# Plain v issued from ScalarE's DMA queue, with a newly searched fixed order, in a fused attention and gated-unit kernel

## The chip, the cores and the metric

The kernel runs on one core of a Trainium2 chip. The metric is the time of one execution on the device, in microseconds. Before the change it is 174.27 us, the median of 3 runs (173.8 to 174.28).

## The reference

Attention over 8 batches, 8 heads, 576 positions and a head width of 64, then a gated unit on its output. Heads 0 to 3 look at the 32 last positions ("plain"), heads 4 to 7 at every fourth of the last 128 ("dilated").

```python
scores = scale * np.matmul(q, k.transpose(0, 1, 3, 2))
mask_plain = (rel >= 0) & (rel < window)
mask_dil = (rel >= 0) & (rel < window * dilation) & (rel % dilation == 0)
...
attn = attn / (np.sum(attn, axis=-1, keepdims=True) + 1e-09)
return np.matmul(attn, v).astype(np.float32)
...
for k in range(K):
    gate_pre += conv_w[k][None, None, :] * xp[:, k:k + S, :]
gate = 1.0 / (1.0 + np.exp(-gate_pre))
val = x @ w_val
return (gate * val @ w_out).astype(np.float32)
```

x is the attention's output with its heads side by side (512 wide), xp the same with K - 1 = 4 rows of zeros ahead, so the gate is a causal convolution of 5 taps in each channel.

## The kernel before, in words

The kernel is a list of 733 tasks, each a handful of instructions of one engine. It is built by `dilated`, `plain`, `gated`, `outputs` and `weights`; no scheduler runs at build time. The string ORDER gives the order of all tasks: an entry such as 34A is task 34 on ScalarE; P is TensorE, V VectorE, G GpSimd, S SyncE. Every engine executes its own entries in that order and waits in order: an instruction that waits holds up all behind it. A number behind the P (33P6) is a count of warm-up matmuls of 512 columns (L659) that are issued ahead of the task. HOMES says which buffer of its class each tensor gets. Both strings were made offline by a planner with assumed costs for each task; the kernel only replays them.

The tasks of one batch b, for the dilated and the plain half:

| name | engine | what |
|---|---|---|
| Lqd, Lkd, Lvd, Lqp, Lkp | SyncE | loads of q, k, v, 576 to 768 KB each |
| Lvp (L302) | SyncE | load of plain v into a buffer vp (two of them), in rows of 64 floats, 256 bytes; 576 KB for batches 0 to 3, 768 KB for 4 to 7 |
| Tqd, Tkd, Tqp, Tkp | TensorE | transposes of q and k to PSUM (L464, L401) |
| Eqd, Ekd, Eqp, Ekp | ScalarE or VectorE | their copies to SBUF (L312, L314) |
| Sd, Sp; Ed, Ep; Md, Mp | TensorE; ScalarE; VectorE | scores (L333), exponential (L340), mask (L347) |
| U | GpSimd or ScalarE | cast of dilated v, vd to vn, 1536 elements a partition (L316) |
| HA, HB, HC, HD | GpSimd or ScalarE | casts of plain v, vp to vw, moved to other partitions: 2, 3, 3 and 2 instructions (batches 0 to 3 only; L316, L312) |
| Ad, Ap; Nd, Np | TensorE; VectorE | attention times v (L356), division by the sum (L365, L366) |
| Xd, Xp; Fd, Fp | TensorE; ScalarE or VectorE | transposes of the result, copies into xT |

For each pair of batches follow the gated unit in 3 or 4 blocks: C (the convolution as matmuls with diagonal matrices, L530), G (its tanh on ScalarE), V (times w_val, L548), Y (VectorE); then 36 output tiles O (times w_out, L577) with their eviction EO and store ST (SyncE). w_val and w_out are loaded as FP32 and cast on GpSimd by Wv and Wo (two tasks for w_out: Wo1, Wo0); O0 needs both. `weights` also makes conv_diag, the identity times conv_w (L616).

Loads on SyncE are kept short by DEPTH = 5: a big load waits until the big load five places earlier has landed.

```python
if t.load:
    t.after = big[-DEPTH] if len(big) >= DEPTH else None
    if t.big:
        big.append(t)
```

Task numbers used below: 49, 114, 203 are Lvp of batches 0, 1, 2; 17 is Lvd and 18 U of batch 0 (U0); 50 to 53 are HA to HD of batch 0, 204 to 207 those of batch 2 (HA2 to HD2); 66 and 76 are the two Ap of batch 0; 178, 181, 190 and 193 the four Ed of batch 2; 209 and 210 the two Eqp of batch 2; 12 and 10 are Wo1 and Wo0; 221 and 231 the two Np of batch 2; 625 is O0.

Of the kernel before, what the change touches and what calls it, by code (L numbers as in the profile page):

```python
# [31 lines left out]
388P 389A 358P 296V 360A 311P 312A 361P 363A 333V 359V 287P 362V 288V 297P 337P 298A 338V 385S 417S 374P 375A
319P 386S 320A 307P 308A 353P 351P 639S 377P 364P 354V 376V 313P 357S 469S 642S 416S 352A 378A 379V 365A 402P
321P 390P 314V 403V 407P 367P 322V 649P 366V 368A 391A 380P 309P 485P 408A 650A 381V 369V 310V 404P 392P 393A
405A 486V 646P 370P 647A 422P 419P 394V 371V 424V 423A 421A 645S 470S 651S 633S 502S 418S 655P 382P 438P 409V
395P 420A 439A 387G 396A 315P 316A 449P 656A 383V 406V 410P 652P 411V 450A 435P 531S 425P 372P 653A 436A 426A
# [672 lines left out]
```

## Time and profile before

| | us | share of the span |
|---|---|---|
| median of 3 runs | 174.27 | |
| the profiled execution | 173.37 | |
| its span, first to last instruction | 171.7 | |
| TensorE (PE) busy | 153.0 | 89% |
| VectorE (DVE) busy | 121.7 | 71% |
| ScalarE (ACT) busy | 108.4 | 63% |
| GpSimd (POOL) busy | 44.2 | 26% |
| DMA: packets' time of 16 engines | | 82.2% |
| granted TensorE clock | 0.998 | |

The profile is of one execution. Busy time leaves out the instructions that issue a DMA; a row "SPq ... DMA_DIRECT2D" tells when SyncE took up an issue and for how long. A share of the DMA engines above 1 means that packets overlap on an engine. In a group's row stand the line, engine, operation, what is written and read with shapes, the count, the busy time in us, the mean of one in ns, and the idle time of the engine ahead of it with what ended most of it.

### The profile page before, as it was taken

To read this page: it belongs to the slowest core of one execution; us is meant where nothing else is said; L and a number is where in the kernel's file an instruction comes from. 1 tells how busy PE (TensorE), PEld (TensorE's weight loads), DVE (VectorE), ACT (ScalarE), POOL (GpSimd) and SP (SyncE) were. 2 spreads that over 40 slices of the span, in tenths; PEclk is the share of its full clock that TensorE was granted. 3 is DMA by queue.
4 is the path that set the end of the run, shared out by engine and by line. 5 is a ranking of instruction groups with operands and counts; after the bars stand their busy time and mean duration, and the time that the engine had idled before them with its cause. 6 is when DMAs were issued, how large, how long until landed. Compare 5 with 4: busy or idle time off the path is not lost.

```text
span 171.7 us, 5752 instructions
## 1 busy us (share of the span) xinstructions
PE 153.0 (89%) x2441; PEld 102.2 (60%) x2460; DVE 121.7 (71%) x243; ACT 108.4 (63%) x182; POOL 44.2 (26%) x82
## 2 busy tenths in 40 slices
PE   6697967888989979899999799989999999999990
PEld 1355654677557546567766567576656577666640
DVE  6549778989899579779788658899368776664220
ACT  2147976198868744798847693888946675242542
POOL 7023998560659427403000000210110000000000
PEclk9999999999999999999999999999999999999999
DMA  4999999999799999999994948969979060333445
GB/s 137 325 355 290 375 370 210 311 374 319 200 383 364 362 269 281 373 353 222 282 328 139 267 115 286 373 165 390 270 202 303 2 244 4 116 119 138 186 165 199
DMA packets 49123, 43.63 MB, mean 254 GB/s; under 512 B 22981, under 2 KB 39365, under 8 KB 49098
## 3 DMA queue, kind: packets, MB, share of 16 engines
q1 hardware_dynamic: 49098, 43.27, 82.2%
q8 instruction: 19, 0.31, 0.7%
q14 instruction: 6, 0.05, 0.1%
HBM read 33.83 MB, written 9.44 MB: 252 GB/s over the span
## 4 chain that ended last, share of the span: by engine, by line
PE 58%; DMA 12%; DVE 11%; ACT 6%; SPq 5%; issue 3%; POOL 3%; ACTq 0%; DVEq 0%; POOLq 0%
PE pu L577 17%; PE pd L548 14%; PE pd L530 9%; DMA qk<-in_k_dram 5%; PE pd L356 5%; DVE et L347 4%; DMA wt<-in_moe_w_out_dram 4%; SPq L281 4%; PE pd L333 4%; DMA qk<-in_q_dram 3%; PE pu L464 3%; POOL w_out L316 3%; PE pd L401 2%; PE pu L488 2%; ACT et L340 2%
## 5 line engine op out<-in xcount | busy, mean ns | idle before, releaser
L340 ACT ACTIVATE et<-pd 128x576 bf16<-128x576 f32 x64 | 39.3, 657 | 10.4 <-PE pd L333 9.3
L347 DVE TENSOR_TENSOR et<-et,mask 128x576 bf16<-128x576 bf16 x64 | 33.9, 557 | 4.7 <-ACT et L340 4.5
L548 PE MATMUL pd<-xT,w_val 128*128 128x384 bf16 (+1 forms) x208 | 34.9, 313 | 0.7 <-DVE xn L366 0.4
L577 PE MATMUL pu<-w_out,yT 128*128 128x512 bf16 x127 | 33.4, 379 | 1.4 <-issue 0.6
L558 DVE SCALAR_TENSOR_TENSOR yT<-gate,pd 128x768 bf16<-128x768 bf16 (+1 forms) x26 | 23.0, 886 | 12.5 <-PE pd L548 8.5
L366 DVE TENSOR_TENSOR xn<-pd,rec 96x768 bf16<-96x768 f32 x32 | 30.5, 954 | 1.1
L316 POOL CAST vn<-vd 128x1536 bf16<-128x1536 f32 x8 | 12.3, 1540 | 70.3 <-DMA vd<-in_v_dram 70.3
L540 ACT ACTIVATE gate<-pd 128x768 bf16<-128x768 f32 (+1 forms) x26 | 19.9, 769 | 10.9 <-DVE yT L558 5.5
L548 PEld LDWEIGHTS <-w_val 128*128 128x128 bf16 x208 | 19.4, 97 | 11.6 <-issue 1.5
L530 PE MATMUL pd<-xT,conv_diag 64*64 64x384 bf16 (+1 forms) x520 | 23.1, 313 | 1.8 <-DVE xT L314 1.1
L584 ACT ACTIVATE osb<-pu 128x512 f32<-128x512 f32 x27 | 16.2, 601 | 11.0 <-PE pu L577 10.7
L577 PEld LDWEIGHTS <-yT 128*128 128x128 bf16 x144 | 12.6, 97 | 13.3 <-issue 1.1
L333 PE MATMUL pd<-qT,kT 64*128 64x96 bf16 x384 | 16.1, 209 | 3.1 <-ACT qT L312 0.9
L530 PEld LDWEIGHTS <-conv_diag 64*64 64x64 bf16 x520 | 15.1, 106 | 6.2 <-issue 2.5
L316 POOL CAST vw<-vp 32x384 bf16<-32x384 f32 (+2 forms) x31 | 16.8, 541 | 7.5 <-DMA vp<-in_v_dram 6.1
L356 PEld LDWEIGHTS <-et 128*128 128x128 bf16 x384 | 14.7, 97 | 6.5 <-DVE et L347 2.5
L464 PE MATMUL pu<-ident,qk 128*128 128x128 bf16 x160 | 14.8, 230 | 3.0 <-DMA qk<-in_k_dram 2.0
L333 PEld LDWEIGHTS <-kT 64*128 64x128 bf16 x384 | 10.1, 96 | 11.5 <-issue 6.3
L464 PEld LDWEIGHTS <-qk 128*128 128x128 bf16 x160 | 10.8, 102 | 7.3 <-DMA qk<-in_k_dram 3.0
L314 DVE COPY xT<-pu 128x576 bf16<-128x576 bf16 x18 | 10.1, 568 | 4.0 <-PE pu L488 3.1
L312 ACT COPY xT<-pu 128x576 bf16<-128x576 bf16 x14 | 8.9, 646 | 6.2 <-PE pu L428 3.6
L365 DVE RECIPROCAL rec<-pd 96x12 f32<-96x12 f32 x32 | 7.1, 223 | 7.6 <-PE pd L356 4.5
(52 smaller groups left out, 146.2 us busy)
## 6 DMA issues: line engine op xcount, KB each, us to landing
out_dram<-osb SPq DMA_DIRECT2D x36, 256.0 KB, 2.7
vd<-in_v_dram SPq DMA_DIRECT2D x8, 768.0 KB, 9.3
qk<-in_k_dram SPq DMA_DIRECT2D x8, 576.0 KB, 7.8
qk<-in_q_dram SPq DMA_DIRECT2D x8, 576.0 KB, 8.0
qk<-in_q_dram SPq DMA_DIRECT2D x6, 640.0 KB, 9.1
qk<-in_k_dram SPq DMA_DIRECT2D x6, 640.0 KB, 8.7
vp<-in_v_dram SPq DMA_DIRECT2D x4, 768.0 KB, 7.9
vp<-in_v_dram SPq DMA_DIRECT2D x4, 576.0 KB, 9.8
```

The costliest lines, as they stand in the source:

```text
L316: nc.gpsimd.tensor_copy(out_, in_)
L333: nc.tensor.matmul(out=ps2[ps.idx][:, l, QB * jj:QB * jj + QB], lhsT=kT[kt.idx][rb, c:c + 128], rhs=qT[qt.idx][rb, c:c + QB], start=True, ...
L340: nc.scalar.activation(out=et[e.idx][:, 0:2 * HW].rearrange("p (l n) -> p l n", l=2), in_=ps2[ps.idx][:, :, 0:HW], func=AF.Exp, scale=scale)
L347: (nc.vector if eng == DVE else nc.gpsimd).tensor_tensor(out=ev, in0=ev, in1=m, op=ALU.mult)
L356: nc.tensor.matmul(out=ps2[po.idx][:, hf, (2 * jj + l) * DA:(2 * jj + l + 1) * DA], lhsT=et[es[hf].idx][:, c:c + 128], rhs=val(j, l), star ...
L366: nc.vector.tensor_tensor(out=xn[xt.idx][0:QB].rearrange("p (h j) l d -> p h (j l) d", h=2), in0=a[:, :, :, 0:D], in1=rr[:, :, :, None].to ...
L464: nc.tensor.transpose(out=o[:, f:f + 128], in_=a[:, c * RD + 128 * cb:c * RD + 128 * cb + 128], identity=ident)
L530: nc.tensor.matmul(out=dst(ps2[pc.idx][64 * ob:64 * ob + 64, n, 0:wd]), lhsT=conv_diag[rb, 2 * cp + n, kk, :], rhs=mov(2 * cp + n, rb, c0 ...
L540: nc.scalar.activation(out=gate[gt.idx][:, :, 0:wd], in_=ps2[pc.idx][:, :, 0:wd], func=AF.Tanh, scale=0.5)
L548: nc.tensor.matmul(out=dst(ps2[pv.idx][:, n, 0:wd]), lhsT=w_val[:, mc, c * 128:(c + 1) * 128], rhs=mov(mc, slice(0, 128), c0), start=(mc = ...
L558: nc.vector.scalar_tensor_tensor(out=yT[yb.idx][:, 2 * cp:2 * cp + 2, t0:t0 + wd], in0=gate[gt.idx][:, :, 0:wd], scalar=1.0, in1=ps2[pv.id ...
L577: nc.tensor.matmul(out=ps1[po.idx], lhsT=yT[yb.idx][:, c, c0:c0 + 128], rhs=w_out[:, c, :], start=(c == 0), stop=(c == NCH - 1))
```

## The change

Plain v is issued by `nc.scalar.dma_start` on ScalarE instead of SyncE, so an Lvp is an entry of ScalarE (49A, 114A, 203A) and stands in ScalarE's order. It no longer counts in the list behind DEPTH, and has no DEPTH wait of its own. ORDER and HOMES are new. The last numbers in SHIFTS, planned costs of the casts HA to HD, go from 1.0 and 1.45 to 1.1 and 1.65; they act through ORDER only. conv_w becomes FP32. New tasks K (the convolution on GpSimd and VectorE) exist for blocks listed in PCONV, and the list is empty, so none is made; with it empty, V still follows its C.

What stands where in the two orders, around the places that matter:

| engine | before | after |
|---|---|---|
| SyncE, first loads | Lkd0 Lc Lqd0 Lkp0 Lvd0 Lqp0 Lvp0 Lqd1 Lwv0 Lkd1 | Lqd0 Lkd0 Lc Lqp0 Lkp0 Lvd0 Lkd1 Lwv0 Lqd1 |
| SyncE, batch 2 on | Lqd2 Lkd2 Lqp2 Lqd3 Lkp2 Lvd2 Lvp2 Lkd3 Lwo1 Lwo0 | Lkp2 Lqd2 Lkd2 Lvd2 Lqp2 Lwo1 Lkd3 Lqd3 Lwo0 |
| ScalarE, start | Ekd0 Eqd0 Ed0 Eqd0 Ed0 Ed0 Ed0 Eqp0 Eqp0 HA0 Ep0 | Eqd0 Lvp0 Ed0 Ed0 Ed0 Eqp0 U0 Ekp0 Ep0 Ed0 Ep0 HB0 Ep0 Ep0 HD0 |
| ScalarE, batch 2 | Ed2 Eqd2 Ed2 Eqp2 Ed2 Ed2 Ekp2 Ekp2 Ep2 G010 Eqd3 HC2 HD2 | Ekd2 Ekd2 Ed2 Ed2 Ed2 Ed2 Eqp2 Lvp2 G010 Ep2 Ep2 Eqd3 Ep2 HB2 G020 Ep2 HA2 |
| GpSimd | U0 HB0 HD0 HC0 ... U2 HB2 HA2 Wo1 Wo0 | HA0 HC0 ... U2 Wo1 HC2 HD2 Wo0 |
| TensorE, around O0 | Ap2 Xd2 Sd3 Ap2 O0 O1 | Ap2 Ap2 Tkd3 O0 Sd3 O1 |

Over the whole order VectorE's copies go from 6 to 12 (Ekd), 3 to 4 (Eqp), 18 to 23 (Fd and Fp), and its output evictions from 9 to 7; ScalarE has the rest. Warm-up matmuls go from 16 to 25.

```diff
-0G 15S 16S 1S 13S 33P6 14S 34A 48S 17S 47S 49S 2P 31P1 32A 3V 18G 38P2 57P 51G 21P 59V 22V 53G 58V 52G 39A 40V
-19P 35P 20A 26P2 36A 23P 80S 27A 37V 24A 28V 25V 41P2 54P 56A 4S 55A 42V 29P 30V 70P 81S 6G 45P3 5G 43P 50A
-60P 73P 7S 46V 71A 44A 74A 8G 112S 61A 96P 84P 63P 64A 149P 72V 97A 75V 76P 98P 85V 65V 62V 82S 66P 77V 86P
-67V 150A 99A 100P 78P 87A 101A 83G 103P 88P 89A 79V 68P 69V 104A 113S 105V 119P 114S 120A 91P 92A 145P 151P
-93V 102V 90V 121A 94P 169S 146A 152V 106P 95V 147P 122P 107V 108P 170S 110P 123V 124A 138P 109A 201S 139A 148V
-135P 185P 136A 125P 128P 129A 126A 111V 165P 166A 140V 130V 137V 116G 127V 186V 234S 202S 157P 158A 187P 115G
-118G 117G 141P 171S 175P 176A 188V 192P 193A 131P 142V 132V 173P 172G 174A 189P 190A 208P 209V 210A 143P 133P
-177P 178A 180P 203S 134V 211P 235S 250P 144V 159P 181A 213A 212A 227P 228A 153P 154A 11S 238P 205G 251V 194V
-179V 191V 160V 182V 239A 206A 195P 229V 196V 207A 167P 168V 204G 12G 183P 184V 155P 252P 224P 225A 214P 240P
-215A 9S 253V 156V 199P 254P 241V 255A 226V 217P 218A 161P 230P 197P 162A 200A 324S 267S 236S 216V 219V 245P
-256V 220P 198A 246A 231V 10G 625P 628P 221V 323S 266S 325S 237G 626A 257P 242P 243A 276P 629A 222P 326G 223A
-258A 278A 277V 163P 341P 232P 303P 247V 244V 259V 233V 342V 304A 299P 300A 164V 339P 260P 248P 329P 305P 330A
...
+0G 13S 14S 31P6 19P 15S 16S 1S 32V 20A 47S 48S 33P1 34V 21P 22V 17S 49A 50G 52G 23P1 2P 38P 35P 24A 39A 81S
+36A 54P 4S 55A 80S 7S 18A 57P 3V 58A 63P5 40V 56V 5G 6G 64A 25V 37V 41P 59V 42V 26P 113S 27A 28V 60P 82S 61A
+86P4 62V 29P 87V 30V 65V 51A 73P 98P 74A 70P 99V 71A 112S 75V 72V 43P2 45P 53A 66P2 76P 44A 46V 114A 67V 84P
+8G 85A 202S 96P 149P 97A 77V 150A 100P 68P 69V 101A 103P 91P 78P 122P 79V 102V 83G 104A 88P 92A 145P 89A 151P
+93V 105V 123V 146A 124A 90V 152V 106P 107V 119P 121A 120A 94P 147P 95V 138P 139A 128P 129A 110P 148V 108P 169S
+111V 109V 125P 211P 126A 135P 136A 127V 212A 140V 130V 213V 137V 157P 165P 185P 170S 187P 186V 158A 117G 115G
+116G 118G 166A 171S 201S 141P 142V 175P 188A 176A 173P 192P 193A 174V 131P 132V 180P1 177P 181A 178A 143P
+133P1 189P 190A 208P 11S 235S 144V 134V 153P 234S 179V 182V 209V 172G 210A 203A 191V 154A 217P2 183P 159P 218A
+224P 184V 194V 160V 227P 252P 225A 250P 253V 251A 12G 228A 195P 196V 155P 156V 229V 214P 205A 161P 199P 162A
+219V 200V 226V 215A 9S 204A 267S 167P 254P 206G 207G 168V 197P 276P 238P 255A 236S 266S 216V 10G 239V 230P
+231V 220P 221V 198A 240P 625P 626V 278A 257P 241A 628P 277A 245P 258A 237G 242P 629A 273P 243A 222P 259V 324S
+256V 329P 223V 330V 246A 323S 325S 260P 261V 275A 268A 326G 163P 341P 274A 232P 164V 233V 247V 271G 269G 270G
...
 DEPTH = 5
+PCONV = []
 NAT = 4
 
 
@@ -141,7 +142,7 @@
             assert eng in t.eng and not t.done and all(d.done for d in t.deps)
             for x in t.tens:
                 assert held.setdefault((x.cls, x.idx), x) is x
-            if t.load:
+            if t.load and eng == SP:
                 t.after = big[-DEPTH] if len(big) >= DEPTH else None
                 if t.big:
                     big.append(t)
@@ -219,7 +220,7 @@
     ident2 = consts.tile([128, D], BF16, name="ident2")
     ident_f = consts.tile([8, 8], FP32, name="ident_f")
     mask = [consts.tile([128, HW], BF16, name=f"mask{i}") for i in range(3)]
-    conv_w = consts.tile([128, NCH, K], BF16, name="conv_w")
+    conv_w = consts.tile([128, NCH, K], FP32, name="conv_w")
     conv_diag = consts.tile([128, NCH, K, D], BF16, name="conv_diag")
     w_val = consts.tile([128, NCH, Dm], BF16, name="w_val")
     w_out = consts.tile([128, NCH, Dm], BF16, name="w_out")
@@ -262,8 +263,8 @@
         nc.vector.memset(mask[1][0:80, QB + 48:2 * QB], 0.0)
 
 
-    def load(name, ten, issue, deps=(), big=True):
-        return plan.add(name, (SP,), lambda e: issue(), deps=deps, tens=[ten], load=True, big=big)
+    def load(name, ten, issue, deps=(), big=True, eng=SP):
+        return plan.add(name, (eng,), lambda e: issue(), deps=deps, tens=[ten], load=True, big=big)
 
     def load_p(src, b, ten, what):
         def issue():
@@ -299,13 +300,13 @@
                 o, a = vp[ten.idx][:, 0:18, 0:D], [[D, 128], [128 * D, 18], [1, D]]
             else:
                 o, a = vp[ten.idx][:, :, 0:D], [[D, 128], [QB * D, 4 * NB], [1, D]]
-            return nc.sync.dma_start(out=o, in_=src_ap(v, (b * H * S - (0 if nat else W)) * D, a))
-        return [load(f"Lvp{b}", ten, issue)]
-
-    SHIFTS = (("HA", ((1, 0, 64, 64, 0), (1, 64, 64, 0, 1)), 1.0),
-              ("HB", ((0, 0, 32, 96, -1), (0, 32, 32, 0, 0), (0, 64, 32, 32, 0)), 1.45),
-              ("HC", ((0, 96, 32, 64, 0), (2, 0, 32, 32, 1), (2, 32, 32, 64, 1)), 1.45),
-              ("HD", ((2, 64, 32, 96, 1), (2, 96, 32, 0, 2)), 1.0))
+            return nc.scalar.dma_start(out=o, in_=src_ap(v, (b * H * S - (0 if nat else W)) * D, a))
+        return [load(f"Lvp{b}", ten, issue, eng=ACT)]
+
+    SHIFTS = (("HA", ((1, 0, 64, 64, 0), (1, 64, 64, 0, 1)), 1.1),
+              ("HB", ((0, 0, 32, 96, -1), (0, 32, 32, 0, 0), (0, 64, 32, 32, 0)), 1.65),
+              ("HC", ((0, 96, 32, 64, 0), (2, 0, 32, 32, 1), (2, 32, 32, 64, 1)), 1.65),
+              ("HD", ((2, 64, 32, 96, 1), (2, 96, 32, 0, 2)), 1.1))
 
     def copy(eng, out_, in_):
         if eng == ACT:
@@ -519,7 +520,8 @@
                 return o.rearrange("p (h t) -> p h t", h=2) if both else o
 
             for cp in range(2):
-                pc, gt, pv = Ten("ps2"), Ten("gate"), Ten("ps2")
+                slow = [g, k, cp] in PCONV
+                pc, gt, pv = Ten("wt" if slow else "ps2"), Ten("gate"), Ten("ps2")
 
                 def conv(eng, cp=cp, pc=pc, c0=c0, mov=mov, dst=dst, wd=wd):
                     for kk in range(K):
@@ -532,14 +534,42 @@
                                     lhsT=conv_diag[rb, 2 * cp + n, kk, :],
                                     rhs=mov(2 * cp + n, rb, c0 + kk - (K - 1)),
                                     start=(kk == 0), stop=(kk == K - 1))
-                t_c = plan.add(f"C{g}{k}{cp}", (PE,), conv,
-                               deps=[x_done[(b, 2 * cp + n)] for b in last for n in range(2)] + [w_ready["conv"]],
-                               tens=[pc, gt, xb], out=pc)
-
-                def th(eng, pc=pc, gt=gt, wd=wd):
-                    nc.scalar.activation(out=gate[gt.idx][:, :, 0:wd], in_=ps2[pc.idx][:, :, 0:wd],
+                ka = Ten("wt")
...
+                c_deps = [x_done[(b, 2 * cp + n)] for b in last for n in range(2)] + [w_ready["conv"]]
+                if slow:
+                    t_c = [plan.add(f"K{'ab'[n]}{g}{k}{cp}", (POOL, DVE), lambda e, n=n, taps=taps: taps(e, n),
+                                    deps=c_deps, tens=[pc, gt, xb, ka]) for n in range(2)]
+                    t_c.append(plan.add(f"Kc{g}{k}{cp}", (DVE,), last_tap, deps=t_c[1:], tens=[pc, gt, xb, ka]))
+                else:
+                    t_c = [plan.add(f"C{g}{k}{cp}", (PE,), conv,
+                               deps=c_deps, tens=[pc, gt, xb], out=pc)]
+
+                def th(eng, pc=pc, gt=gt, wd=wd, slow=slow):
+                    a = wt[pc.idx][:, 0:2 * GW].rearrange("p (n t) -> p n t", n=2) if slow else ps2[pc.idx]
+                    nc.scalar.activation(out=gate[gt.idx][:, :, 0:wd], in_=a[:, :, 0:wd],
                                          func=AF.Tanh, scale=0.5)
-                t_g = plan.add(f"G{g}{k}{cp}", (ACT,), th, deps=[t_c], tens=[pc, gt])
+                t_g = plan.add(f"G{g}{k}{cp}", (ACT,), th, deps=t_c, tens=[pc, gt])
 
                 def val(eng, cp=cp, pv=pv, c0=c0, mov=mov, dst=dst, wd=wd):
                     for n in range(2):
@@ -551,7 +581,7 @@
                                 rhs=mov(mc, slice(0, 128), c0),
                                 start=(mc == 0), stop=(mc == NCH - 1))
                 t_v = plan.add(f"V{g}{k}{cp}", (PE,), val,
-                               deps=[x_done[(b, c)] for b in last for c in range(NCH)] + w_ready["val"] + [t_c],
+                               deps=[x_done[(b, c)] for b in last for c in range(NCH)] + w_ready["val"] + (t_c if not slow else []),
                                tens=[pv, xb], out=pv)
 
                 def stt(eng, cp=cp, pv=pv, gt=gt, t0=t0, wd=wd):
```

More of the change, by code (lines that the diff above doesn't have):

```diff
@@ L32 @@
[L32 to L36, printed above, removed]
@@ L534, in conv, with taps @@
                                     start=(kk == 0), stop=(kk == K - 1))
[L535 to L540 removed]
+                ka = Ten("wt")
+                def taps(eng, n, c=2 * cp, pc=pc, ka=ka, c0=c0, mov=mov, dst=dst, wd=wd):
+                    acc = dst((wt[ka.idx] if n else wt[pc.idx])[:, 0:wd])
+                    tmp = dst(wt[ka.idx][:, GW:GW + wd])
+                    for kk in range(K - n):
+                        x = mov(c + n, slice(0, 128), c0 + kk - (K - 1))
+                        w = conv_w[:, c + n, kk:kk + 1]
+                        if kk and eng == DVE:
+                            nc.vector.scalar_tensor_tensor(out=acc, in0=x, scalar=w, in1=acc, op0=ALU.mult, op1=ALU.add)
+                            continue
+                        e = nc.vector if eng == DVE else nc.gpsimd
+                        e.tensor_scalar(out=tmp if kk else acc, in0=x, scalar1=w, scalar2=None, op0=ALU.mult)
+                        if kk:
+                            e.tensor_tensor(out=acc, in0=acc, in1=tmp, op=ALU.add)
@@ new lines, in last_tap @@
+                def last_tap(eng, c=2 * cp + 1, pc=pc, ka=ka, c0=c0, mov=mov, dst=dst, wd=wd):
+                    for lo, to in ((0, 64), (64, 0)):
+                        nc.vector.scalar_tensor_tensor(
+                            out=dst(wt[pc.idx][to:to + 64, GW:GW + wd]), in0=mov(c, slice(lo, lo + 64), c0),
+                            scalar=conv_w[lo:lo + 64, c, K - 1:K], in1=dst(wt[ka.idx][lo:lo + 64, 0:wd]),
+                            op0=ALU.mult, op1=ALU.add)
+                c_deps = [x_done[(b, 2 * cp + n)] for b in last for n in range(2)] + [w_ready["conv"]]
```

39 lines of the change are left out of this document (22 added, 17 removed).

## The prediction

> **What bounds the kernel now.** I read the page first, then the busy time of each engine by stage, then SyncE's own timeline, then TensorE's gaps.
>
> ```profile
> PE 153.0 (89%) x2441; PEld 102.2 (60%) x2460; DVE 121.7 (71%) x243; ACT 108.4 (63%) x182; POOL 44.2 (26%) x82
> ```
>
> TensorE is busy for 153.0 of 171.7 us, so a new order can win at most a part of what is left. Where that lies is in the table by stage (the columns are busy time and instructions of PE, PEld, DVE, ACT and POOL, then clock, DMA share, GB/s):
>
> ```profile
> 24.00:58.00 34.00, 29.67 (x547) 20.67 (x548) 30.19 (x51) 24.29 (x42) 20.32 (x39) 1.00 1.02 315
> 58.00:113.00 55.00, 50.66 (x854) 35.00 (x861) 41.53 (x75) 38.83 (x66) 10.13 (x12) 1.00 0.93 275
> 113.00:168.00 55.00, 54.27 (x800) 35.28 (x805) 33.62 (x60) 31.65 (x54) 1.47 (x1) 1.00 0.58 178
> ```
>
> TensorE idles 4.3 us in 24 to 58, 4.3 us in 58 to 113 and 0.7 us after that. So the last 55 us can only get worse. In 24 to 58 VectorE is busy 30.19 of 34 us, more than TensorE, and the DMA engines are full. That stage has three resources near their limit, and the order decides there.
>
> SyncE's timeline shows what the change aims at: L302 is the load of plain v, and the row behind each is the next issue.
>
> ```profile
> 22.43 0.37 SPq L302 DMA_DIRECT2D vp<-in_v_dram  x1
> 23.82 5.13 SPq L281 DMA_DIRECT2D qk<-in_q_dram  x1
> ...
> 36.78 0.37 SPq L302 DMA_DIRECT2D vp<-in_v_dram  x1
> 38.26 5.67 SPq L281 DMA_DIRECT2D qk<-in_k_dram  x1
> ```
>
> A plain v load is issued in 0.37 us, but the issue after it takes 5.13 and 5.67 us. What moved on the DMA engines meanwhile:
>
> ```profile
> 16.00:26.00 10.00, 7.65 (x170) 5.63 (x171) 7.70 (x15) 8.55 (x16) 9.39 (x27) 1.00 1.07 373
> 27.00:28.50 1.50, 1.42 (x19) 0.74 (x12) 1.02 (x3) 1.50 (x3) 1.50 (x4) 1.00 1.33 243
> 28.00:31.00 3.00, 1.96 (x31) 1.31 (x30) 2.96 (x5) 0.71 (x1) 1.28 (x1) 1.00 0.67 129
> 43.50:46.00 2.50, 2.50 (x38) 1.36 (x35) 2.27 (x3) 1.89 (x4) 1.61 (x1) 1.00 0.48 109
> ```
>
> 373 GB/s in an ordinary stretch, 243 while a plain v load drains (256-byte rows), then a hole: 129 GB/s over 3.0 us and 109 over 2.5 us. The holes lose 3.0 x (1 - 129/373) = 2.0 us and 2.5 x (1 - 109/373) = 1.8 us of transfer. Whether that is time of the kernel is seen at TensorE's gaps (in brackets, with what ended them):
>
> ```profile
> 22.46 0.45 PE L464 MATMUL pu<-ident,qk 128*128 128x128 bf16 x5 [1.01 <-DMA qk<-in_k_dram]
> ...
> 30.01 0.92 PE L356 MATMUL pd<-vn,et 128*128 128x65 bf16 x24 [1.04 <-DVE et L347]
> 34.49 0.43 PE L333 MATMUL pd<-qT,kT 64*128 64x96 bf16 x12 [0.65 <-ACT kT L312]
> ...
> 42.61 0.69 PE L401 MATMUL pd<-ident,qk 128*64 128x128 bf16 x18 [0.61 <-ACT qT L312]
> ```
>
> Only the first ends with a transfer. The three that follow the first hole, 2.3 us together, end with VectorE and ScalarE; a load that comes sooner helps them only through those queues.
>
> **The change part by part: the start.** Two things stand differently. U0, the cast of the first dilated v, moves from GpSimd to ScalarE, and its load stands behind plain q and k instead of plain k alone.
>
> ```profile
> 11.98 1.47 POOL L316 CAST vn<-vd 128x1536 bf16<-128x1536 f32 x1 [7.65 <-DMA vd<-in_v_dram]
> ...
> 22.75 0.35 PE L356 MATMUL pd<-vw,et 128*128 128x65 bf16 x6
> ```
>
> The load was there at 11.98. One plain load more ahead (576 KB at 373 GB/s, 1.6 us) makes it 13.5; if the whole plain v from ScalarE's queue goes first (576 KB at 243 GB/s, 2.4 us) it is 15.9. ScalarE waits for it in order, and behind U0 stand one copy, five exponentials (one of the dilated half) and the five casts of HB0 and HD0, which the first Ap0 needs.
>
> ```profile
> L340 ACT ACTIVATE et<-pd 128x576 bf16<-128x576 f32 x64 | 39.3, 657 | 10.4 <-PE pd L333 9.3 <-DVE xn L366 1.0
> L312 ACT CAST vw<-vp 32x384 bf16<-32x384 f32 x7 | 3.6, 517 | 0.1
> ```
>
> That is U0 (no ScalarE row; 1.5 us as on GpSimd, at most 4 x 0.517 = 2.1 by the 384-element cast; I take 1.5, the row of the same shape) + 6 x 0.657 (the copy priced like an exponential) + 5 x 0.517 = 8.0 us. HD0 ends at 21.5 to 23.9. Before, the second Ap0 started at 22.75, held up by the 1.01 us wait for dilated k of batch 1 that stood between the two; now they follow each other, the second some 0.6 us behind HD0, at 22.1 to 24.5. Against 22.75: -0.6 to +1.8, and I take **+0.6**, the middle.
>
> **The middle: plain v of batch 2 and O0.** Load 203 now stands on ScalarE behind Eqp2 (210), and GpSimd's order became Wo1, HC2, HD2, Wo0. So the second half of the cast w_out waits for a plain v that is issued late, and O0, the first output matmul, waits for w_out. TensorE has the same 82 tasks ahead of O0 in both orders but for one (a transpose of 18 instead of a score group of 6).
>
> ```profile
> 41.92 0.64 ACT L312 COPY qT<-pd 128x576 bf16<-128x576 bf16 x1 [0.56 <-DVE qT L314]
> 42.46 1.20 ACT L340 ACTIVATE et<-pd 128x576 bf16<-128x576 f32 x2
> ...
> DMA to landing us min/median/max: 5.8/9.1/11.2
> ...
> L316 POOL CAST vw<-vp 32x384 bf16<-32x384 f32 x21 | 11.5, 547 | 2.0 <-DMA vp<-in_v_dram 1.0
> ...
> 52.80 0.61 POOL w_out L316
> ...
> 56.36 0.38 PE pu L577
> ```
>
> Before, Eqp2 (41.92) had two exponentials behind it, done at 43.66; now all four stand ahead, so Eqp2 ends where they ended: 43.7 + 0.6 from the start = 44.3. The issue takes 0.37 (SyncE's rows above; ScalarE has none), so 44.7. From issue to landing a plain v took 5.8 to 11.2 us behind SyncE's other loads. Now it need not queue, but shares: the lowest row holds 2.4 us of its own transfer, and at half the rate it would be 2.4 more, 8.2; since that row has some queueing in it too, I take the middle of 5.8 and 8.2, 7.0: 51.7. HC2 and HD2 are five casts, 5 x 0.547 = 2.7; Wo0 to O0 took 56.36 - 52.80 = 3.6. O0 starts at 58.0 instead of 56.36: **+1.6**, with the start's 0.6 in it. With 5.8 and the start's -0.6 it is -0.8; with 11.2 and its +1.8 it is +7.0. The Trainium skill speaks for the upper side. Its page "DMA: Bandwidth & Descriptors", section "Queues, rings and completion order", says that each DMA engine changes between queues packet by packet, a packet being some 9 to 17 descriptors. A packet of 256-byte rows is then small beside one of 1 to 2 KB rows, and plain v gets less than half: with a fifth of the bytes against 1 KB rows (an estimate by that page) some 2.3 MB of other loads pass with it, which at the rates above is 6.2 + 2.4 us of transfer where I have 4.8, and the sum would be 3.8 more, +5.4. No trace of before has two such queues at work.
>
> **VectorE.** By the counts of both orders it takes over six copies of kT, one of qT and five of xT, and gives two output evictions to ScalarE.
>
> ```profile
> L314 DVE COPY xT<-pu 128x576 bf16<-128x576 bf16 x18 | 10.1, 568 | 4.0 <-PE pu L488 3.1 <-PE pu L428 0.5 <-ACT et L340 0.3
> L586 DVE TENSOR_SCALAR osb<-pu 128x512 f32<-128x512 f32 x9 | 6.2, 685 | 2.2 <-PE pu L577 2.2
> L314 DVE COPY kT<-pu 128x576 bf16<-128x576 bf16 x6 | 2.7, 446 | 0.0
> L314 DVE COPY qT<-pd 128x576 bf16<-128x576 bf16 x3 | 2.3, 750 | 0.0
> ```
>
> 6 x 0.446 + 0.750 + 5 x 0.568 - 2 x 0.685 = +4.9 us, of which four tasks, some 2 us, stand ahead of the last Np2 (58 us). In 24 to 58 it had 3.8 us idle. This delays the same point as O0, so the later of the two counts, not their sum: 0 to +2.2, taken as 0 beside +1.6; if it is the later one, that is a rival below.
>
> **ScalarE** gets eight issues (8 x 0.37 = 3.0), U0 (1.5), one more cast (0.5) and two evictions (some 1.4, as on VectorE), and loses the twelve copies (12 x 0.657 = 7.9): -1.5 us in all. It idles 9.7, 16.2 and 23.4 us in the three stages, which covers the issues; without that cover they would cost their 3.0.
>
> ```profile
> L577 PE MATMUL pu<-w_out,yT 128*128 128x512 bf16 x127 | 33.4, 379 | 1.4 <-issue 0.6
> ```
>
> **Nothing** for the rest: nine more warm-up matmuls, as long as these output matmuls of 512 columns (33.4/127 = 0.26 us each), stand before instructions that wait, and cost 2.4 us if those don't wait; conv_w in FP32 makes the product with the identity at most twice as long, and it runs while TensorE waits for the first loads; the conv on the vector engines is planned for no block.
>
> **After O0** TensorE's idle time is 4.3 + 0.7 us. I take it as unchanged: loads come sooner, VectorE has 2.9 us more to do and 13.5 us idle in 58 to 113. Bounds: -2.5 to +2.5.
>
> **Sum.** The profiled execution took 173.37 us for its span of 171.7, and 173.37 + 1.6 = 175.0. The three runs' median is 174.27, 0.9 above that execution, so I forecast **175.9** on the median's scale. The ends of the O0 term give 173.5 to 181.3; of these I count 174.8 to 179.3 as this case.
>
> **The rivals.**
> Faster: the holes were the root. Their 2.0 + 1.8 us of transfer come back, w_out is loaded ahead of batch 3 and the three gaps of 2.3 us go, while plain v lands soon enough: 174.27 - 2.3 = 172.0. For it: the gaps follow the first hole; SyncE's 5-us issues must vanish. Against: no gap after 24 us ends with a transfer.
> Slower by another way: VectorE becomes the bound in 24 to 58. It was at 30.19/34 = 0.89; 2 us more work at that share is 2.2 us, with the start's 0.6 it is 2.8: 177.1. It decides once that stage's idle 3.8 us can't be used. Against: VectorE idles 13.5 us just after.
> No change: the DMA engines were the limit in 24 to 58 (share 1.02) and stay it, and TensorE's sum does the rest: 174.3. The Trainium skill's section "Issuing engines are not separate DMA queues" of the same page says so: issuing from several engines saves only the sequencer's issue time, usually small. Here the share agrees that the engines are full, but an issue of 5.67 us is not small.
>
> **How the numbers follow.** Forecast 0.42, VectorE 0.16, faster 0.32, no change 0.10. A change within 0.3% (0.5 us) can't be told from none. So slower 0.58, same 0.10, faster 0.32. Range 171.3 to 179.3: below, the faster case with 0.7 us to spare; above, +5.0, near the long landing.
>
> **What would show it.** Right: no issue of 5 us on SyncE; no hole near 28 and 44 us; U0 on ScalarE ending after 15 us; plain v of batch 2 landing 6 us or more after its issue, with ScalarE or GpSimd idle for it, and O0 later than 56.4 behind w_out's cast; VectorE's busy time up by about 5 us. Wrong: O0 before 56 us, TensorE's idle time in 24 to 113 below 8.6 us, or the start's second Ap0 before 22 us.

## The result, and the profile after

| | before | after |
|---|---|---|
| median, us | 174.06 (4 runs) | 185.92 (4 runs; 185.11 to 189.47) |
| ratio, 95% interval | | 1.0666 [1.061, 1.0723] |
| profiled execution; its span | 173.37; 171.7 | 185.38; 183.7 |
| O0, the first output tile: its first matmul starts | 55.89 | 68.86 |
| from there to the end of the span | 115.8 | 114.8 |

Some executions fall into a slower state (one of the four of after, 189.47, and four of e6's ten): the medians here count them, the ratios leave them out.

The change costs 6.7%, in the profile 12.0 us of span. O0 comes 13.0 us late and what follows takes 1.0 us less than before (183.7 - 68.86 = 114.8, against 171.7 - 55.89 = 115.8). So all of the loss arises ahead of O0. (The 56.36 that the prediction uses for O0 is the start of its second matmul, which waits for the last cast of w_out; in after that one starts at 69.28.) The row of O0 in before's timeline of TensorE:

```profile
55.89 2.14 PE L577 MATMUL pu<-w_out,yT 128*128 128x512 bf16 x7
```

The page of after: span, busy time by engine, the chain that ended last by engine and by line, and the two groups of plain v's loads (count, KB each, median us from issue to landing).

```profile
span 183.7 us, 5779 instructions
...
PE 160.7 (88%) x2469; PEld 104.0 (57%) x2469; DVE 125.2 (68%) x253; ACT 105.6 (58%) x174; POOL 40.4 (22%) x80
...
PE 64%; DMA 20%; ACT 6%; DVE 3%; issue 2%; POOL 1%; SPq 0%; ACTq 0%
PE pu L607 17%; PE pd L578 15%; DMA vp<-in_v_dram 15%; PE pd L532 10%; PE pd L357 5%; PE pd L334 5%; PE pu L465 4%; DMA out_dram<-osb 3%; PE pd L402 3%; PE pu L429 2%; DMA qk<-in_q_dram 2%; PE pu L489 2%; ACT vw L313 2%; ACT et L341 2%; ACT gate L570 1%
...
vp<-in_v_dram ACTq DMA_DIRECT2D x4, 768.0 KB, 6.3
vp<-in_v_dram ACTq DMA_DIRECT2D x4, 576.0 KB, 12.9
```

15% of the chain, some 27 us, is the transfer of plain v itself. Its four loads of the first batches, 576 KB each, take 12.9 us in the middle; the four later ones, a third larger, take 6.3. Where on the chain they stand, in order of time (start, us, what):

```profile
6.32 17.68 DMA vp<-in_v_dram
...
24.49 0.52 ACT vw L313
...
45.86 0.63 POOL vw L317
...
54.02 9.31 DMA vp<-in_v_dram
```

The load of batch 0 is issued at 6.32 and lands 17.7 us later; that of batch 2 is issued only at 54.02 and takes 9.3. In before the same two landed 10.9 and 9.2 us after their issue. The load of batch 1 lies between, and shows in the timelines. ScalarE's, with its DMA issues (ACTq):

```profile
6.32 0.43 ACTq L303 DMA_DIRECT2D vp<-in_v_dram  x1
...
14.17 1.48 ACT L313 CAST vn<-vd 128x1536 bf16<-128x1536 f32 x1 [1.57 <-DMA vd<-in_v_dram]
...
24.01 1.53 ACT L313 CAST vw<-vp 32x320 bf16<-32x320 f32 x3 [5.12 <-DMA vp<-in_v_dram]
...
25.57 0.37 ACTq L303 DMA_DIRECT2D vp<-in_v_dram  x1
```

GpSimd's:

```profile
24.12 2.96 POOL L317 CAST vw<-vp 64x384 bf16<-64x384 f32 x5 [19.78 <-DMA vp<-in_v_dram]
...
42.20 5.95 POOL L317 CAST vw<-vp 32x384 bf16<-32x384 f32 x10 [7.30 <-DMA vp<-in_v_dram]
...
63.48 2.75 POOL L317 CAST vw<-vp 32x384 bf16<-32x384 f32 x5 [11.92 <-DMA vp<-in_v_dram]
66.30 2.92 POOL L317 CAST w_out<-wt 64x512 bf16<-64x512 f32 x4
```

And TensorE's, its gaps and O0 (the last row):

```profile
25.80 0.28 PE L357 MATMUL pd<-vw,et 128*128 128x65 bf16 x4 [2.20 <-POOL vw L317]
27.89 0.29 PE L357 MATMUL pd<-vw,et 128*128 128x65 bf16 x2 [1.81 <-ACT vw L313]
...
48.20 0.22 PE L357 MATMUL pd<-vw,et 128*128 128x65 bf16 x2 [2.61 <-POOL vw L317]
...
65.77 0.30 PE L334 MATMUL pd<-qT,kT 64*128 64x96 bf16 x6 [3.11 <-ACT gate L570]
...
68.86 1.23 PE L607 MATMUL pu<-w_out,yT 128*128 128x512 bf16 x4
```

It is one pattern three times, at 24, 42 and 63 us: a cast engine stands idle until plain v lands (up to 19.8, 7.3 and 11.9 us), then casts, and TensorE waits for what comes of it. For batches 0 and 1 its next matmul with plain v ends its wait with such a cast (the second wait of batch 0 with ScalarE's casts HD0); for batch 2 the gap at 65.77 ends with a gate that stood behind casts of plain v on ScalarE. The waits in total (us, times, longest), on the cast engines and on TensorE behind them:

```profile
POOL vw L317 <- DMA vp<-in_v_dram: 46.8, 4, 19.8
...
ACT vw L313 <- DMA vp<-in_v_dram: 9.4, 2, 5.1
...
PE pd L357 <- POOL vw L317: 4.8, 2, 2.6
...
PEld L357 <- ACT vw L313: 4.4, 2, 2.5
```

In before's answer ScalarE and TensorE have no such row, and GpSimd's is

```profile
POOL vw L316 <- DMA vp<-in_v_dram: 6.1, 4, 2.5
```

By stage (columns as in the prediction's tables):

```profile
24.00:68.00 44.00, 33.28 (x597) 22.78 (x598) 30.28 (x55) 27.76 (x47) 23.18 (x52) 0.92 0.95 301
...
62.00:67.00 5.00, 1.89 (x46) 1.34 (x44) 1.83 (x4) 3.56 (x7) 3.25 (x6) 1.00 0.08 18
...
27.00:28.50 1.50, 0.61 (x12) 0.61 (x13) 1.04 (x2) 1.45 (x3) 1.39 (x6) 0.50 1.05 386
28.00:31.00 3.00, 3.00 (x42) 2.52 (x45) 2.32 (x5) 1.72 (x3) 2.85 (x13) 0.50 1.10 343
43.50:46.00 2.50, 2.09 (x46) 1.33 (x38) 2.50 (x5) 2.43 (x5) 2.27 (x5) 1.00 1.02 369
```

The two holes of before are filled: 343 GB/s where it was 129, and 369 where it was 109. SyncE's issues of 5 us behind a plain v load are gone too. In the stage before O0 TensorE idles 10.7 of 44 us (before: 4.3 of 34), of which 3.1 stand at 62 to 67 us, where the DMA engines have next to nothing to do (18 GB/s). Behind its two waits at 24 to 28 us the granted clock stands at 0.50. The transfers were made smoother, and the kernel got slower.

The rows that each queue moved show why plain v is late. This is a count of the recorded packets, each of which is one row of a load (q1 is SyncE's queue, q10 ScalarE's; per us over the stretch):

```
after       11-13 us   q1 262 rows, mean 1006 B, 263 GB/s   q10 252 rows, 256 B,  64 GB/s
after       30-35 us   q1 249 rows, mean  999 B, 248 GB/s   q10 247 rows, 256 B,  63 GB/s
after       60-62 us   q1  22 rows, mean 1990 B,  44 GB/s   q10 711 rows, 255 B, 181 GB/s
```

While both queues have work, they move about the same number of rows, not of bytes. (How many rows make one turn the records don't show.) Against rows of 1 KB those of 256 bytes get a fifth of the bytes. Only where SyncE's queue has little left, at 60 us (it issues nothing from 53 to 67), do they go at 181 GB/s.

### The profile page after: what moved, and what is told of

Read it like the earlier page. It is cut to its first block, busy times and chain, and to the rows that moved or that the text cites. A ratio compares the mean times of both kernels' runs of the same rounds, so it can differ in the third digit from the quotient of the medians.

```text
span 183.7 us, 5779 instructions
## 1 busy us (share of the span) xinstructions
PE 160.7 (88%) x2469; PEld 104.0 (57%) x2469; DVE 125.2 (68%) x253; ACT 105.6 (58%) x174; POOL 40.4 (22%) x80
## 3 DMA queue, kind: packets, MB, share of 16 engines
q10 hardware_dynamic: 21632, 5.51, 14.9%
## 4 chain that ended last, share of the span: by engine, by line
PE 64%; DMA 20%; ACT 6%; DVE 3%; issue 2%; POOL 1%; SPq 0%; ACTq 0%
PE pu L607 17%; PE pd L578 15%; DMA vp<-in_v_dram 15%; PE pd L532 10%; PE pd L357 5%; PE pd L334 5%; PE pu L465 4%; DMA out_dram<-osb 3%; PE pd L402 3%; PE pu L429 2%; DMA qk<-in_q_dram 2%; PE pu L489 2%; ACT vw L313 2%; ACT et L341 2%; ACT gate L570 1%
## 5 line engine op out<-in xcount | busy, mean ns | idle before, releaser
L348 DVE TENSOR_TENSOR et<-et,mask 128x576 bf16<-128x576 bf16 x64 | 32.8, 537 | 9.9 <-ACT et L341 9.7
L578 PE MATMUL pd<-xT,w_val 128*128 128x384 bf16 (+1 forms) x208 | 35.4, 313 | 0.8 <-DVE xn L367 0.6
L607 PE MATMUL pu<-w_out,yT 128*128 128x512 bf16 x144 | 35.9, 379 | 0.0
L614 ACT ACTIVATE osb<-pu 128x512 f32<-128x512 f32 x29 | 17.3, 600 | 14.6 <-PE pu L607 14.2
L532 PE MATMUL pd<-xT,conv_diag 64*64 64x384 bf16 (+1 forms) x520 | 23.5, 321 | 0.1
L334 PE MATMUL pd<-qT,kT 64*128 64x96 bf16 x384 | 17.2, 213 | 7.1 <-ACT kT L313 3.3
L357 PEld LDWEIGHTS <-et 128*128 128x128 bf16 x384 | 15.6, 100 | 10.4 <-ACT vw L313 4.4
L317 POOL CAST vn<-vd 128x1536 bf16<-128x1536 f32 x7 | 10.2, 1468 | 41.0 <-PE pd L334 22.4
L315 DVE COPY xT<-pu 128x576 bf16<-128x576 bf16 x23 | 13.4, 595 | 7.3 <-PE pu L429 4.6
L532 PEld LDWEIGHTS <-conv_diag 64*64 64x64 bf16 x520 | 14.2, 108 | 5.8 <-issue 1.4
L402 PE MATMUL pd<-ident,qk 128*64 128x128 bf16 x288 | 11.4, 232 | 0.3 <-DVE xn L367 0.2
## 6 DMA issues: line engine op xcount, KB each, us to landing
vp<-in_v_dram ACTq DMA_DIRECT2D x4, 576.0 KB, 12.9
```

Source lines behind the costliest of these rows:

```text
L317: nc.gpsimd.tensor_copy(out_, in_)
L334: nc.tensor.matmul(out=ps2[ps.idx][:, l, QB * jj:QB * jj + QB], lhsT=kT[kt.idx][rb, c:c + 128], rhs=qT[qt.idx][rb, c:c + QB], start=True, ...
L348: (nc.vector if eng == DVE else nc.gpsimd).tensor_tensor(out=ev, in0=ev, in1=m, op=ALU.mult)
L357: nc.tensor.matmul(out=ps2[po.idx][:, hf, (2 * jj + l) * DA:(2 * jj + l + 1) * DA], lhsT=et[es[hf].idx][:, c:c + 128], rhs=val(j, l), star ...
L532: nc.tensor.matmul(out=dst(ps2[pc.idx][64 * ob:64 * ob + 64, n, 0:wd]), lhsT=conv_diag[rb, 2 * cp + n, kk, :], rhs=mov(2 * cp + n, rb, c0 ...
L578: nc.tensor.matmul(out=dst(ps2[pv.idx][:, n, 0:wd]), lhsT=w_val[:, mc, c * 128:(c + 1) * 128], rhs=mov(mc, slice(0, 128), c0), start=(mc = ...
```

## The experiments

Medians are those of the runs of one occasion; "before" beside them was 173.39 for the first four, 173.37 for the next four and 173.9 for the last four.

| | us | ratio to before, 95% |
|---|---|---|
| e1 after, plain v on SyncE | 174.19 | 1.004 [1.0005, 1.0074] |
| e2 before, plain v on ScalarE | 204.88 | 1.1811 [1.1745, 1.1876] |
| e3 after, plain v in rows of 4680 B | 173.89 | 1.0037 [0.9996, 1.0079] |
| e4 after, last cast of w_out first | 184.74 | 1.0641 [1.0587, 1.0694] |
| e5 before, dilated v on ScalarE | 188.13 | 1.082 [1.0757, 1.0884] |
| e6 after, plain v loaded and not waited for | 172.9 | 0.9926 [0.9898, 0.9954] |
| e7 before, plain v in rows of 4680 B | 174.07 | 1.005 [1.0023, 1.0076] |
| e8 e1 without 19 warm-ups | 172.41 | 0.9972 [0.9941, 1.0003] |
| e9 after, plain v in rows of 520 B | 180.81 | 1.0381 [1.032, 1.0441] |
| e10 after, plain v in rows of 1560 B | 176.02 | 1.0106 [1.0045, 1.0168] |
| e11 before without 10 warm-ups | 173.91 | 0.9992 [0.9962, 1.0022] |
| e12 e8 again | 173.47 | 0.9984 [0.9949, 1.002] |

**e1: the new order, with plain v back on SyncE's queue.** In the order's eight entries of Lvp, A becomes S (49A to 49S and so on; as loads of SyncE they count behind DEPTH again), and

```diff
-            return nc.scalar.dma_start(out=o, in_=src_ap(v, (b * H * S - (0 if nat else W)) * D, a))
+            return nc.sync.dma_start(out=o, in_=src_ap(v, (b * H * S - (0 if nat else W)) * D, a))
```

> The changed kernel with the eight plain v loads issued from SyncE again, at the same places of the new order. Theory 'shared engines' (each DMA engine takes one packet from ScalarE's queue and one from SyncE's in turn, so 256-byte rows get a fifth of the bytes beside 1 KB rows): plain v lands 6 to 11 us after its issue as in the kernel before, not 13 to 18, O0 stands near 57 to 61 us instead of 68.9, and the time is 174 to 179 us. Rival 'new order' (VectorE's 5 us more work, U0 on ScalarE, the order itself): the time stays at 183 us or more.

Measured 174.19: of the 6.7% all but 0.4 are gone. The new order, the other warm-ups, the casts' new places and VectorE's extra work together cost at most 0.7%. Plain v lands 6.1 to 11.5 us after its issue, and O0 starts at 57.23, both close to what was expected. From e1's page, its table by stage, SyncE's timeline and GpSimd's:

```profile
PE 157.5 (91%) x2469; PEld 102.0 (59%) x2469; DVE 126.8 (73%) x253; ACT 105.6 (61%) x174; POOL 41.6 (24%) x80
```
```profile
24.00:58.00 34.00, 30.62 (x578) 20.69 (x568) 30.84 (x52) 24.35 (x41) 19.99 (x37) 1.00 1.06 318
```
```profile
22.91 5.31 SPq L271 DMA_DIRECT2D qk<-in_k_dram  x1
...
40.89 5.16 SPq L657 DMA_DIRECT2D wt<-in_moe_w_out_dram  x1
```
```profile
48.16 2.74 POOL L317 CAST vw<-vp 32x384 bf16<-32x384 f32 x5 [3.66 <-DMA vp<-in_v_dram]
50.97 2.83 POOL L317 CAST w_out<-wt 64x512 bf16<-64x512 f32 x4
```

VectorE is busy for 126.8 us, 5.1 more than before, and TensorE still works 30.62 of the 34 us from 24 to 58 (29.67 before). The long issues on SyncE are back, and plain v of batch 2 can be cast at 48.16 instead of 63.48.

**e2: the old order, with plain v on ScalarE's queue.** The eight entries of Lvp go from S to A, `nc.sync` becomes `nc.scalar` as in the change, and the cap on SyncE's queue leaves them out (`if t.load and eng == SP`).

> The kernel before with the eight plain v loads issued from ScalarE at their places of the old order, the rest unchanged. 'Shared engines': plain v of batches 0 to 2 lands 13 to 18 us after its issue, the first Ap0 starts at 24 us or later instead of 20.9, and the time is 179 to 188 us. 'New order': the queue does no harm and the time is 173.5 to 175.5 us.

Measured 204.88, 18% slower and above the 188 that was expected at most: the move harms an order that wasn't searched for it far more. From e2's page, the casts of plain v on GpSimd (busy, mean ns, idle before):

```profile
L316 POOL CAST vw<-vp 32x384 bf16<-32x384 f32 (+2 forms) x31 | 16.3, 525 | 54.7 <-DMA vp<-in_v_dram 41.2
```

On before's page the same row has 7.5 us of idle time, 6.1 of it for plain v. So in both orders the loss comes with plain v on ScalarE's queue. Here it is not the rows alone: plain v of batches 0 and 1 landed 18.1 and 17.0 us after its issue, about as expected, but batch 2's after 7.6, and batches 1 and 2 were issued at 32.44 and 60.97, where SyncE had issued them at 22.43 and 36.78. What such a delay costs is the subject of e5.

**e3: the changed kernel, plain v as one row for each partition.** Queue, places in the order and bytes (but for 2%) stay; 2304 rows of 256 bytes become 128 of 4680.

```diff
-                o, a = vp[ten.idx][:, 0:18, 0:D], [[D, 128], [128 * D, 18], [1, D]]
+                o, a, w0 = vp[ten.idx].rearrange("p n d -> p (n d)")[:, 0:18 * DA], [[18 * DA, 128], [1, 18 * DA]], 0
```

> The changed kernel, plain v still from ScalarE's queue and about as many bytes, but in one row of 4.7 KB (batches 0 to 3) or 6.2 KB (4 to 7) for each partition instead of 18 or 24 rows of 256 bytes; what then stands in plain v's buffer is not plain v in the layout that the attention takes, so the output is another. 'Shared engines' by packets: long rows get more than half of the bytes, plain v lands 4 to 7 us after its issue, and the time is 171 to 178 us. Rival 'second queue' (the queue of ScalarE is late or weak whatever it carries): landing stays above 10 us and the time at 182 us or more. 'New order': 183 us or more with plain v early.

Measured 173.89. In e3, the answer on the tile of plain v, and its queue on the page (packets, MB, share):

```profile
DMA to landing us min/median/max: 4.2/6.1/7.7
```
```profile
q10 hardware_dynamic: 1152, 5.59, 10.3%
```

In after the same answer was 5.5/7.8/17.7, and the queue had 21632 packets. So it isn't the second queue as such that costs 12 us, but the second queue with short rows. This run also parts the late issue from the rows: at the same place of the same order, plain v of batch 2 is issued at 45.85 instead of 54.02, so 8.2 us of that delay were made by the short rows of the batches before. The 6.5 us that are left against e1 (39.37) cost nothing that shows, as the two kernels take the same time.

**e9 and e10: the same with rows of 520 and 1560 bytes**, between the two (`"p (n m) d -> p n (m d)"` with m = 2 and 6, so 9 and 3 rows for each partition).

> The kernel after with plain v fetched in rows of 520 bytes, 1152 rows per load instead of 2304 of 256 bytes, still on ScalarE's queue and at its places in the order (the plain v data lands in another layout, so the output is not the reference's; the bytes read grow by 2% for the spare column). Theory: the two queues take turns row by row, so plain v now gets 520/(520+1024), a third of the bytes instead of a fifth, and needs half the turns. In the kernel after 2304 rows took 13.6 us from the first packet at 10.4 us to the landing at 23.99, 170 a us; 1152 rows at 170 to 227 a us are 5.1 to 6.8 us: first plain v landed at 15.5 to 17.2 (after: 23.99), the time near that of after with plain v on SyncE, 174 to 177 us. Rival: the second queue gets a fixed part of the bytes, or ScalarE issues too late: the row length changes nothing, landing near 24 us and 183 to 186 us.

> The same with rows of 1560 bytes, 384 rows per load. Theory: 384 turns beside rows of 1 KB, at 350 GB/s for 2.6 KB per turn some 135 a us, 2.8 us: first plain v landed at 13 to 14.5, the time as with rows of 4680 bytes, 173.5 to 174.5 us. Together with 256, 520 and 4680 bytes the landing should fall with the number of rows. Rival: no dependence on the row, 183 to 186 us.

Measured 180.81 and 176.02, 3.8 and 1.5 us above what was expected at most, and in the order of the row lengths. The count of rows on ScalarE's queue, for the load of batch 0 (16 small packets stand beside the rows of each load) and, per us, in a stretch where both queues have work:

```
rows of    packets   issue   first row   last row   | stretch, us    q1 rows, GB/s    q10 rows, GB/s | median us
 256 B       2320     6.32     10.31      23.19     |  11 to 13       262    263       252     64   |  185.92
 520 B       1168     6.35     10.14      18.10     |  11 to 13       220    220       218    113   |  180.81
1560 B        400     6.32     10.01      13.73     |  11 to 12       146    150       144    225   |  176.02
4680 B        144     6.07      9.75      12.22     |  10.5 to 11.5    74     76        75    351   |  173.89
```

The transfer shrinks from 12.9 to 8.0, 3.7 and 2.5 us as the rows get fewer, for nearly the same bytes. At every length the counts of the two queues are equal within 4%, and the bytes go with the row: at 520 bytes 1:2, at 4680 bytes more than 4:1 for plain v. What was expected of the first landing, 15.5 to 17.2 and 13 to 14.5 us, came out at 18.64 and 14.28. At 520 bytes 95% of the packets were through by 15.80; the last 5% took until 18.10. Why these come so late stays open.

**e4: the last cast of w_out ahead of plain v's casts.** In the changed order 10G moves up:

```diff
-219V 200V 226V 215A 9S 204A 267S 167P 254P 206G 207G 168V 197P 276P 238P 255A 236S 266S 216V 10G 239V 230P
+219V 200V 226V 215A 9S 10G 204A 267S 167P 254P 206G 207G 168V 197P 276P 238P 255A 236S 266S 216V 239V 230P
```

> The changed kernel with GpSimd's second cast of w_out (Wo0) ahead of HC2 and HD2 instead of behind them, nothing else. The prediction's step (O0 waits for w_out behind plain v's casts): O0 comes 2 to 3 us sooner and the time falls by 2 to 3 us. 'Shared engines' as read in the trace (both Ap2, ahead of O0 in TensorE's order, wait for ScalarE's casts of the same late plain v until 67.3 us, and Wo0 ends at 69.2): O0 comes 0 to 0.6 us sooner and the time falls by less than 1 us.

From e4, GpSimd's timeline (the last four of its seven casts of w_out are the moved ones) and TensorE's, with O0:

```profile
48.74 4.55 POOL L317 CAST w_out<-wt 128x512 bf16<-128x512 f32 x7
62.92 2.98 POOL L317 CAST vw<-vp 32x384 bf16<-32x384 f32 x5 [9.63 <-DMA vp<-in_v_dram]
```
```profile
68.29 1.03 PE L607 MATMUL pu<-w_out,yT 128*128 128x512 bf16 x4
```

w_out is cast 16 us sooner, by 53.3 instead of 69.2, and O0 starts at 68.29 instead of 68.86, as much sooner as the casts of plain v ahead of it (62.92 instead of 63.48). The ratio, 1.0641 beside 1.0666, is the same within the intervals. w_out was not what O0 waited for: ahead of O0 on TensorE stand the two Ap2, and these need plain v of batch 2.

**e5: the old order, with dilated v (rows of 1 KB) on ScalarE's queue.** As e2, for the entries of Lvd.

> The kernel before with the dilated v (768 KB in rows of 1 KB) issued from ScalarE at the places of its order, plain v left on SyncE. 'Shared engines, row by row': rows of 1 KB beside rows of 1 to 2.3 KB get a third to a half of the bytes, dilated v lands 6 to 11 us after its issue, and the time is 173 to 179 us, far from the 204.9 of plain v in the same place. Rival 'any load on ScalarE's queue hurts, because it leaves the order of SyncE': 185 us or more.

Measured 188.13, far outside the 173 to 179 of the first theory and within what its rival said. From e5, the waits, and the issues in ScalarE's timeline:

```profile
POOL vn L316 <- DMA vd<-in_v_dram: 97.5, 8, 27.4
...
PE pd L356 <- POOL vn L316: 11.6, 4, 5.0
```
```profile
41.37 0.46 ACTq L290 DMA_DIRECT2D vd<-in_v_dram  x1
...
63.76 0.38 ACTq L290 DMA_DIRECT2D vd<-in_v_dram  x1
...
64.94 0.57 ACTq L290 DMA_DIRECT2D vd<-in_v_dram  x1
```

GpSimd waits for dilated v in before too (70.3 us in 7 waits); new are the 27 us more, and that TensorE waits behind them, for which before has no row. SyncE issued these three loads at 33.38, 49.37 and 53.99 in before; on ScalarE, which works its order off one by one, they stand behind exponentials and copies and are issued 8.0, 14.4 and 11.0 us later, in a kernel that by then runs late itself. They landed 11.8, 5.1 and 6.1 us after that, where SyncE's queue took 10.8, 8.3 and 9.4 in before. So with rows of 1 KB the landing was no worse on the whole, and by this trace there is a second price, apart from the rows: a load on a compute engine's queue leaves when that engine gets to it. No run takes this price alone. In the changed kernel e3 bounds it: with long rows it costs nothing that shows.

**e6: the changed kernel, plain v loaded into buffers that nothing reads.** The casts take a constant from vp instead; the load, its queue and its rows stay.

```diff
-                o, a = vp[ten.idx][:, 0:18, 0:D], [[D, 128], [128 * D, 18], [1, D]]
+                o, a = vx[ten.idx][:, 0:18, 0:D], [[D, 128], [128 * D, 18], [1, D]]
```

> The changed kernel with every plain v load on ScalarE's queue as it is, but into two spare buffers that nothing reads; the casts and matmuls take a constant in plain v's place. The DMA engines carry the same rows and SyncE's waits stay, only the waits for plain v's data go. 'Consumers wait' (the time is lost where casts and then TensorE wait for plain v): 173 to 177 us. Rival 'SyncE's loads are held back' (the other loads get fewer bytes and wait for plain v's semaphores): 181 us or more.

Measured 172.9. The same rows go over the same queue, the loads land as late (17.3, 15.2 and 16.6 us after their issue for batches 0 to 2), SyncE still waits 5.5 us for them, and nothing of the loss is left. So what the other loads and SyncE lose by sharing doesn't show in the time; the loss is made by those who need plain v.

**e7: the old order and queue, with e3's long rows.**

> The kernel before with plain v in one row of 4.7 or 6.2 KB for each partition instead of rows of 256 bytes, on SyncE as before; what then stands in plain v's buffer is not plain v in the layout that the attention takes, so the output is another. SyncE's issues of 5 us and the holes of the transfers behind them should go. The prediction's faster rival ('the holes are the root'): 171 to 172.5 us where before has its 174. 'Transfers are not what ends last': within 0.6 us of before.

From e7, the table by stage where before had its holes:

```profile
28.00:31.00 3.00, 2.23 (x32) 1.51 (x32) 2.93 (x7) 0.00 (x0) 1.86 (x5) 1.00 1.09 361
43.50:46.00 2.50, 2.50 (x48) 1.67 (x47) 2.50 (x5) 1.69 (x3) 2.25 (x5) 1.00 1.09 371
```

Both holes are gone, with the issues of 5 us (the longest from 15 to 50 us takes 1.94, for two), and the time is 174.07, 0.7 us above before's 173.37, just outside the 0.6 of the second theory and away from the first. Filling the holes gains this kernel nothing.

**e8, e11 and e12: without the later warm-ups.** In e1's order and in the old one the digit behind P in the entries goes (33P1 to 33P), but for the first six warm-ups.

> The kernel of e1 (new order, plain v on SyncE) without the 19 warm-up matmuls behind the first six. If they only fill waits, as the prediction took them, the time stays within 0.7 us of e1's 174.2 (ratio to before 1.000 to 1.008). Rival 'they take TensorE's time': 1 to 3 us less than e1 (ratio 0.986 to 0.998).

> The kernel before without the ten warm-up matmuls that stand after its first six (1, 2, 2, 2 and 3 at five places up to about 20 us). If they cost what they did in the new order (19 fewer took 1.0% off), ten fewer are worth some 0.5%: 172.5 us. Rival: before's ten stand where TensorE waits anyway: 173.4, no change. Should the matmuls behind them then find a lower clock, it is slower, 174.

> A second measurement, on another occasion, of the new order with plain v on SyncE and without the 19 later warm-ups, which gave 0.9972 (0.9941 to 1.0003). If the gain is real, 0.994 to 0.999 again; if it was chance, 1.000 to 1.004, as with the warm-ups.

e8 came out at 0.9972; measured again it was 0.9984, within what was expected of a real gain, but with an interval on both sides of 1 as the first. The old order without its ten is at 0.9992. So no kernel without the later warm-ups differs from before by a margin that can be told. Both readings of the new order lie some 0.6% under e1's 1.004, measured on another occasion; whether its 19 warm-ups cost that 1 us stays open.

## Why the prediction was wrong

The direction was right and so was the kind of cause: plain v alone on ScalarE's queue lands late, a cast engine waits for it, O0 moves. The size was not, 185.92 against 175.9 and an upper end of 179.3.

- **The step that failed** is the start, which had plain v's load of batch 0 as 2.4 us of transfer at most and no wait for its landing: HB0 and HD0 ran straight behind U0. For batch 1 there was no term at all. Measured, that load took 12.9 us from its first row to its last and landed 17.7 us after its issue, batch 1's 16.5 (10.9 and 9.1 in before). U0 did as predicted (load there at 14.2, within 13.5 to 15.9; 1.48 us, from 1.5), but HB0 then waited 5.1 us, to 24.01, for plain v. The second Ap0 started at 28.3, not 22.1 to 24.5.
- **Why the landing was late.** "At half the rate it would be 2.4 more" takes the queues to share by bytes. They share by rows, and plain v's rows are the short ones: 64 GB/s beside 263. The prediction's sentences on the Trainium skill's page "DMA: Bandwidth & Descriptors", section "Queues, rings and completion order", had the kind of sharing right: each DMA engine goes round the queues by packet. The equal counts of rows agree with it, and the estimate of a fifth of the bytes is what was measured. It was given for batch 2, as the upper side, and not counted in the forecast.
- **The one landing that was priced**, batch 2's, came out nearer: 9.3 us with the issue, not 7.4. There SyncE's queue had little left from 60 us on: after 3.9 us to its first row the transfer took 5.0 us.
- **What the sum missed.** The prediction's 56.36 is O0's second matmul, so the sum goes to the second matmul of after, at 69.28. Load 203 was issued at 54.02, 9.7 us after the 44.3 of the prediction; it landed 9.3 us later instead of 7.4, 1.9 more; from there it was 69.28 - 63.34 = 5.9 instead of 6.3, 0.4 less. 9.7 + 1.9 - 0.4 = 11.2, and 58.0 + 11.2 = 69.2. Of the 9.7, 5.0 were there at the second Ap0 (28.3 - 23.3); the other 4.7 came up to the issue, with batch 1's wait and the lower clock among them.
- **The gate was another.** O0's first matmul waited behind the two Ap2, not behind w_out's cast (e4); its second waited for that cast, some 0.2 us more. As both hang on the same landing, this hardly moved the sum.
- **VectorE** nearly as predicted: 4.9 us more work forecast, 3.5 measured in after and 5.1 in e1, taken as no cost; the rival that made it the bound (+2.8 us) falls with e1's +0.8.
- **After O0** nearly unchanged, as taken: 114.8 against 115.8 us.
- **Nothing for the rest** held for conv_w: the product with the identity took 1491 ns, before 1492. For the nine more warm-ups it is open (e8, e12).
- **The faster rival** falls. Its conditions stand together in e3: no issue of 5 us, no hole (353 and 362 GB/s at 28 to 31 and 43.5 to 46 us), and plain v of batch 2 landed 10 us sooner than in after; its time is before's, not 2.3 us less. e7 has the first two in the old order and gains nothing. What the prediction held against it, that no gap after 24 us ended with a transfer, was the better reading.
- **No change** falls as well. Issuing from another engine made 11.7 us of difference between e1 and after, as it is also another place in the turn. The Trainium skill's page "DMA: Bandwidth & Descriptors" says in its section "Issuing engines are not separate DMA queues" that it saves only the time of the issue; the runs differ from that, and they decide.

Not tried: the changed kernel with its loads of plain v earlier in ScalarE's order and their short rows kept, which would show the late issue by itself.

## What to carry to other kernels

Before a load goes to a queue of its own, compare its rows with those of the loads that run beside it: the queues took turns by rows, so the load with the shorter rows got the smaller part of the bytes, and it should be one that nobody needs soon. A load on a compute engine's queue also leaves no sooner than that engine reaches it (e5: 8 to 14 us later than on SyncE). And a hole in the transfers is worth nothing until a gap of the bounding engine ends with a transfer; e7 fills the holes for no gain, and after fills them for a loss.

## What the hardware showed that was not expected

- On ScalarE's queue 3.6 to 4.0 us passed from the issue to the first recorded row, whatever its length, while SyncE's queue was busy (6.32 to 10.31, 25.57 to 29.40 and 54.02 to 57.92 in after, 6.07 to 9.75 in e3); for each of the last four loads of after it was 1.0 us (as 112.61 to 113.65). For three of these SyncE's queue moved nothing in that time; for the last it moved 222 rows, so a busy queue alone doesn't explain it. The cause stays open.
- TensorE idled about 4 us within 23.6 to 27.9, and its granted clock stood at 0.50 from 27 to 33: the convolution's matmuls (L532) took 523 ns each up to 31 us, 321 on average over the run. So the wait was followed by slower work; that it lowered the clock isn't tested.
